# Top-k attention and a hard-swish MLP on one core: another pipeline for the weight conversion, wider PSUM tiles for transposes, another order at the end of a step

## The chip, the cores and the metric

The kernel runs on one core of one Trainium2 chip. The metric is the time of one execution on the device, in microseconds (us). The engines are named as the profile names them: PE (TensorE, with PEld for its weight loads), DVE (VectorE), ACT (ScalarE), POOL (GpSimd) and SP (SyncE, which here only issues DMAs).

## The reference

```python
scores = scale * np.matmul(q, k.transpose(0, 1, 3, 2))          # q, k, v: (8, 8, 576, 64) float32
kth = np.partition(scores, -top_k, axis=-1)[..., -top_k:-top_k + 1]   # top_k = 32
scores = np.where(scores >= kth, scores, -1000000000.0)
attn = np.exp(scores - np.max(scores, axis=-1, keepdims=True))
attn = attn / (np.sum(attn, axis=-1, keepdims=True) + 1e-09)
x = np.matmul(attn, v)            # then (B,H,S,D) -> (4608, 512)
h = x @ w_in                      # w_in (512, 2048) float64
g = h * np.clip(h + 3.0, 0.0, 6.0) / 6.0
out = (g @ w_out).astype(np.float32)     # w_out (2048, 512) float64
```

## The kernel before, in words

The weights arrive as float64, and no engine reads that, so the kernel takes each number as two 32-bit words and puts a float32 together. `convert` does this for one chunk of 128 x 512 numbers, and there are 32 chunks: 16 of `w_in`, then 16 of `w_out`. It loads the words into a tile `st` (two buffers), ACT takes the magnitude of the high word (`Abs`) and scales the low word, POOL clamps, DVE shifts and masks the bits, POOL multiplies and adds, and DVE (`finish`, L125) puts the sign in. `finish` reads `st` too, so `st` is given back only there.

The attention is cut into 160 units: for each of the 8 batches, five tiles of query rows (four of 128, one of 64, the "rest"), and for each tile four pairs of heads. A unit has two rows of 576 scores on each partition (a rest unit has one: the two heads lie on the two halves of the partitions). There is one loop over steps `n`, and all engines take their instructions in the order in which the loop writes them. Step `n` works on several units at once:

- PE computes the scores of unit n+1 into PSUM (`ps`), and ACT copies them to SBUF (`sc`).
- DVE finds the 32 largest of unit n in four rounds, `top(0)` to `top(3)`: each round finds the 8 largest (MAX8), and the first three rounds strike them out (MATCH_REPLACE8).
- POOL masks unit n (`mask`: two passes L246, an add L251, and the shift for the exponential L254).
- ACT does the exponential of unit n-1 (`exp`, L259), and POOL adds a small number to its sums (`den`, L264).
- DVE takes the reciprocal of unit n-2 (L268), ACT scales by it (`weights`, L270), PE transposes the result in nine blocks of 128 x 128 (L282, L291), and ACT copies the blocks to SBUF (`eT`, L284, and `rT`, L410).
- In odd steps PE multiplies two units by v (`values`, L304), and ACT copies the result (`xT`).

Every four units of a query tile make one tile of 128 tokens, and for it `feed_forward` is put on a list. It has eight pieces: four pieces `h` (32 PE passes each, then ACT's relu L329, then a DVE "gate" L333) and four pieces `acc` (the second matmul). `piece()` takes the next one off the list. There are two slots for a piece in a step, one ahead of the transposes and one behind them, and a third in every fourth step. A rest step has one or two.

PSUM has 8 banks. Before, `ps_sc` has 3, `ps_tr` two tiles of 1 bank (the blocks of a unit go through it in two halves, and the transposed k and q of a pair of heads in three parts), `ps_rt` 1 and `ps_w` 2.

Of the kernel before, what the change touches and what calls it, by code (L numbers as in the profile page):

```python
# [11 lines left out]
U32 = mybir.dt.uint32  # L12
PSUM = bass.MemoryType.PSUM
# [12 lines left out]
def kernel(  # L26
# [18 lines left out]
    W2 = 2 * S  # L45
# [14 lines left out]
    rtpool = pool("rt", 2)  # L60
# [7 lines left out]
    ps_tr = pool("ps_tr", 2, space=PSUM)  # L68
    ps_rt = pool("ps_rt", 1, space=PSUM)
# [9 lines left out]
    nc.vector.memset(three[:], 3.0)  # L79
    w_in = const([P, NHP, FF], "w_in")  # L80
# [17 lines left out]

    def convert(dst, src):

        st = stpool.tile([P, 2 * WC], U32, tag="st", name="st")
        nc.sync.dma_start(st[:], src)
        words = st[:].rearrange("p (n two) -> p n two", two=2)
        lo, hi = words[:, :, 0], words[:, :, 1]
        cv = cvpool.tile([P, 3, WC], F32, tag="cv", name="cv")
        a, s, f = cv[:, 0, :], cv[:, 1, :], cv[:, 2, :]
# [22 lines left out]

        return finish  # L130
# [13 lines left out]
    class Pair:  # L144
# [28 lines left out]
        def transpose(self):  # L173
            kT = self.kT = kqpool.tile([P, JP], F32, tag="kT", name="kT")
            qT = self.qT = kqpool.tile([P, S], F32, tag="qT", name="qT")
            for src, dst in ((self.kin, kT[:]), (self.qin, qT[:, 0:JP])):
                ps = ps_tr.tile([P, 512], F32, tag="tr", name="kq")
                for j in range(J):
                    rows = src[:, j, :, :].rearrange("p h d -> p (h d)")
                    nc.tensor.transpose(ps[:, j * P : (j + 1) * P], rows, ident[:])  # L180
                nc.scalar.copy(dst, ps[:, 0:JP])  # L181
            ps = ps_tr.tile([P, 512], F32, tag="tr", name="kq")
            for i, src in enumerate((self.kin, self.qin)):
                rows = src[0:R, J, :, :].rearrange("p h d -> p (h d)")
                nc.tensor.transpose(ps[:, i * R : (i + 1) * R], rows, ident[0:R, 0:R])
            for hh in range(2):
                d = slice(hh * D, (hh + 1) * D)
                nc.scalar.copy(self.kr[d, hh, :], ps[d, 0:R])
            nc.scalar.copy(qT[:, JP:S], ps[:, R : 2 * R])

    class Unit:
# [10 lines left out]
        def scores(self):  # L202
# [5 lines left out]
            sc = self.sc = scpool.tile([P, W2], F32, tag="sc", name="sc")  # L208
# [7 lines left out]
            else:  # L216
                nc.tensor.matmul(ps[:, 0:JP], pr.qT[h0, qs], pr.kT[h0, :])  # L217
                nc.tensor.matmul(ps[:, S + R : 1024], pr.qT[h1, qs], pr.kT[h1, 0 : 1024 - S - R])  # L218
                nc.tensor.matmul(ps[:, 1024:W2], pr.qT[h1, qs], pr.kT[h1, 1024 - S - R : JP])
                nc.tensor.matmul(ps[:, JP : S + R], pr.qT[:, qs], pr.kr[:].rearrange("p h r -> p (h r)"))  # L220
                nc.scalar.copy(sc[:], ps[:, 0:W2])  # L221

# [51 lines left out]
        def transpose(self, rt):  # L274

            sc = self.sc
            eT = self.eT = etpool.tile([P, 2 * J, P], F32, tag="eT", name="eT")

            def blocks(dst, starts):
                ps = ps_tr.tile([P, 512], F32, tag="tr", name="tr")  # L280
                for i, c0 in enumerate(starts):
                    nc.tensor.transpose(ps[:, i * P : (i + 1) * P], sc[:, c0 : c0 + P], ident[:])  # L282
                n = len(starts) * P
                nc.scalar.copy(dst.rearrange("p c q -> p (c q)"), ps[:, 0:n])  # L284

            main = [c * P for c in range(J)]
            blocks(eT[:, 0:J, :], main)
            if self.rest:
                blocks(eT[:, J : J + 2, :], [JP, S - P])
            else:  # L290
                nc.tensor.transpose(rt, sc[:, JP : JP + P], ident[:])  # L291
                blocks(eT[:, J : 2 * J, :], [S + R + c0 for c0 in main])

        def values(self, dst, rT):
# [90 lines left out]
    chunks = [(dst, src) for dst, src in weight_chunks()]  # L385
    finishes = []

    def convert_some(n):
        for dst, src in chunks[:n]:
            finishes.append(convert(dst, src))  # L390
            if len(finishes) > 1:
                finishes.pop(0)()
        del chunks[:n]
        if not chunks:
            while finishes:
# [139 lines left out]
```

## Time and profile before

| what | value |
|---|---|
| median of 3 runs | 2212.35 us (2211.54 to 2212.62) |
| the profiled execution | 2209.28 us |
| its span, first to last instruction | 2207.5 us |
| PE, DVE, ACT, POOL busy | 1697.8, 1612.1, 999.7, 1216.6 us |
| mean granted PE clock | 0.94 of full speed |

Busy times are sums over the whole span; whether an engine sets the end in a stretch is read from the views of that stretch. Everything between the span and the time of the execution (1.8 us) lies outside the program's instructions.

### The profile page before, as it was taken

Reading aid. Unit: us, or ns where it says so; the run is one execution under the profiler, and the core shown is the slowest. Engines: PE = TensorE matmul, PEld = TensorE weight load, DVE = VectorE, ACT = ScalarE, POOL = GpSimd, SP = SyncE. Lnnn points to the kernel's source line nnn. Section 1 sums busy time; section 2 is a strip of 40 time slices with the busy share of each in tenths; the row PEclk is TensorE's granted clock in tenths of the full one; section 3 lists DMA queues with packets and bytes.
Section 4 is the critical chain, followed back from the end, with each engine's and each line's share of the span. In section 5 each row is a group of like instructions: output and inputs, shape, how many; then the busy total and the mean of one; then the engine's idle time right before and its main releaser. Section 6 shows DMA issues by size and latency. Waiting matters only on the chain.

```text
span 2207.5 us, 31292 instructions
## 1 busy us (share of the span) xinstructions
PE 1697.8 (77%) x11904; PEld 1227.9 (56%) x11904; DVE 1612.1 (73%) x3313; ACT 999.7 (45%) x1893; POOL 1216.6 (55%) x918
## 2 busy tenths in 40 slices
PE   3012042588999989898989899988999898988989
PEld 2011032366666666665666666666666666656665
DVE  4555544577888888868888878768888888688880
ACT  2122222244455555544555555544554555445542
POOL 3554544555555656555656565646566665555651
PEclk9975566799999999999999999999999999999999
DMA  4111111101000001001000100001000110000000
GB/s 118 48 38 54 48 39 54 40 6 38 22 22 6 22 26 35 9 17 43 22 6 16 27 22 22 6 22 38 22 6 22 30 34 6 6 6 5 6 6 10
DMA packets 101142, 56.55 MB, mean 26 GB/s; under 512 B 84096, under 2 KB 92288, under 8 KB 100992
## 3 DMA queue, kind: packets, MB, share of 16 engines
q1 hardware_dynamic: 100992, 54.55, 9.1%
q8 instruction: 94, 1.54, 0.3%
q14 instruction: 56, 0.46, 0.1%
HBM read 45.09 MB, written 9.44 MB: 25 GB/s over the span
## 4 chain that ended last, share of the span: by engine, by line
PE 64%; DVE 10%; POOL 9%; issue 8%; ACT 4%; DMA 4%; SPq 0%; ACTq 0%; POOLq 0%
PE h L321 21%; PE acc L340 19%; PE pv L304 7%; PE tr L282 7%; POOL sc L251 4%; POOL wk L246 3%; DVE m L232 3%; PE ps L217 3%; DVE wk L236 3%; PE ps L220 2%; DMA st<-in_moe_w_out_dram 2%; DMA st<-in_moe_w_in_dram 2%; PE ps L218 1%; PE rt L291 1%; DVE w_in L125 1%
## 5 line engine op out<-in xcount | busy, mean ns | idle before, releaser
L246 POOL TENSOR_SCALAR wk<-sc,m 128x576 f32<-128x576 f32 x288 | 636.4, 2218 | 613.2 <-DVE m L232 613.2
L232 DVE MAX8 m<-wk 128x8 f32<-128x576 f32 x864 | 613.0, 746 | 1.6
L282 PE MATMUL tr<-ident,sc 128*128 128x128 f32 x1216 | 195.2, 290 | 467.5 <-issue 390.0
L340 PE MATMUL acc<-w_out,g 128*128 128x512 f32 x1152 | 523.5, 598 | 0.0
L321 PE MATMUL h<-xT,w_in 128*128 128x128 f32 x4096 | 481.5, 276 | 0.0
L321 PEld LDWEIGHTS h<-xT,w_in 128*128 128x128 f32 x4096 | 469.2, 193 | 1.6 <-issue 0.5
L282 PEld LDWEIGHTS tr<-ident,sc 128*128 128x128 f32 x1216 | 147.0, 148 | 533.2 <-issue 472.6
L236 DVE MATCH_REPLACE8 wk<-m,wk 128x576 f32<-128x576 f32 x576 | 423.8, 743 | 0.0
L251 POOL TENSOR_TENSOR sc<-sc,wk 128x1152 f32<-128x1152 f32 (+1 forms) x160 | 382.1, 2388 | 13.3
L340 PEld LDWEIGHTS acc<-w_out,g 128*128 128x128 f32 x1152 | 208.9, 191 | 215.8 <-issue 214.2
L329 ACT ACTIVATE g<-h,three 128x512 f32<-128x512 f32 x144 | 98.9, 687 | 371.6 <-PE h L321 371.6
L270 ACT ACTIVATE sc<-sc,den 128x576 f32<-128x576 f32 x288 | 208.1, 766 | 129.9 <-DVE den L268 129.8
L333 DVE SCALAR_TENSOR_TENSOR g<-g,h 128x512 f32<-128x512 f32 x144 | 98.5, 684 | 194.6 <-ACT g L329 194.6
L284 ACT COPY eT<-tr 128x512 f32<-128x512 f32 x320 | 176.5, 566 | 110.0 <-PE tr L282 101.2
L259 ACT ACTIVATE sc<-sc,shift 128x576 f32<-128x576 f32 x288 | 220.8, 770 | 0.0
L221 ACT COPY sc<-ps 128x1152 f32<-128x1152 f32 x128 | 142.1, 1110 | 159.4 <-PE ps L220 158.4
L232 DVE MAX8 m<-sc 128x8 f32<-128x576 f32 x288 | 203.8, 744 | 13.7 <-ACT sc L221 11.4
L236 DVE MATCH_REPLACE8 wk<-m,sc 128x576 f32<-128x576 f32 x288 | 211.8, 742 | 0.0
L268 DVE RECIPROCAL den<-den 128x2 f32<-128x2 f32 (+1 forms) x160 | 26.0, 162 | 195.6 <-POOL den L264 195.4
L304 PE MATMUL pv<-eT,vm 128*64 128x128 f32 (+1 forms) x2560 | 161.0, 270 | 0.0
L217 PE MATMUL ps<-kT,qT 64*128 64x512 f32 x256 | 151.7, 674 | 0.8 <-ACT qT L181 0.8
L304 PEld LDWEIGHTS pv<-eT,vm 128*64 128x64 f32 x2560 | 133.9, 141 | 13.2 <-issue 9.0
(62 smaller groups left out, 1466.4 us busy)
## 6 DMA issues: line engine op xcount, KB each, us to landing
kin<-in_k_dram SPq DMA_DIRECT2D x64, 128.0 KB, 3.0
qin<-in_q_dram SPq DMA_DIRECT2D x64, 128.0 KB, 2.9
vm<-in_v_dram SPq DMA_DIRECT2D x64, 128.0 KB, 2.3
st<-in_moe_w_in_dram SPq DMA_DIRECT2D x16, 512.0 KB, 3.9
st<-in_moe_w_out_dram SPq DMA_DIRECT2D x16, 512.0 KB, 3.6
out_dram<-o SPq DMA_DIRECT2D x32, 256.0 KB, 2.3
kin<-in_k_dram SPq DMA_DIRECT2D x32, 32.0 KB, 2.6
qin<-in_q_dram SPq DMA_DIRECT2D x32, 32.0 KB, 2.4
```

Source lines behind the costliest of these rows:

```text
L217: nc.tensor.matmul(ps[:, 0:JP], pr.qT[h0, qs], pr.kT[h0, :])
L232: nc.vector.max(self.m[:, t, 8 * r : 8 * r + 8], self.cur[t])
L236: nc.vector.match_replace(wk, self.m[:, t, 8 * r : 8 * r + 8], self.cur[t], LOWEST)
L246: nc.gpsimd.tensor_scalar(self.wk[:, t, :], self.row[t], self.m[:, t, TOP_K - 1 : TOP_K], DROP, ALU.is_lt, ALU.mult,)
L251: nc.gpsimd.tensor_tensor(both, both, self.wk[:, 0:nt, :].rearrange("p t s -> p (t s)"), ALU.add)
L259: nc.scalar.activation(self.row[t], self.row[t], AF.Exp, bias=self.shift[:, t : t + 1], scale=scale, accum_out=self.den[:, t : t + 1],)
L270: nc.scalar.activation(self.row[t], self.row[t], AF.Copy, scale=self.den[:, t : t + 1])
L282: nc.tensor.transpose(ps[:, i * P : (i + 1) * P], sc[:, c0 : c0 + P], ident[:])
L284: nc.scalar.copy(dst.rearrange("p c q -> p (c q)"), ps[:, 0:n])
L304: nc.tensor.matmul(dst[hh * D : (hh + 1) * D, :], pr.vm[:, hh, c, :] if c < J else pr.vr[:, hh, :], rhs, start=(c == 0), stop=(c == J),)
L321: nc.tensor.matmul(h[:, (f - f0) * P : (f - f0 + 1) * P], w_in[:, i, f * P : (f + 1) * P], xT[:, i, :], start=(i == 0), stop=(i == NHP - 1),)
L340: nc.tensor.matmul(acc[:], gs[f // 4][:, (f % 4) * P : (f % 4 + 1) * P], w_out[:, f, :], start=(f == 0), stop=(f == NFC - 1),)
```

## The change

Four things change.

1. **The conversion.** `convert` becomes a generator of two parts with one chunk in flight. The first part loads `st`, has ACT take the magnitude, POOL clamp it, and ACT write the sign (as 2.0 or -2.0) and the scaled low words into PSUM. The second part, one `convert_step()` later, is four DVE operations (shift, xor with the sign, mask, multiply by the low words) and one POOL add, which writes the weights. No instruction of the second part reads `st`. `convert_step()` stands three times in the loop (ahead of `top(1)`, `top(2)` and the end of the step), three times ahead of it, and once more in step 0, instead of three chunks in a row at each step's end.
2. **PSUM for transposes.** `ps_tr` is one tile of 3 banks (`wide()`), one buffer, for the nine blocks of a unit, for the ten transposes of a pair, and for the sign and low words of a chunk. `ps_rt` and the `rT` tile are gone; one ACT copy of 1152 columns takes all nine blocks.
3. **Scores.** Three matmuls per unit instead of four, the narrow one first, and two ACT copies instead of one.
4. **Order.** `weights` (DVE's reciprocal, ACT's two scalings) moves to the head of the step, ahead of `top(0)` and of the first piece. `exp` now stands ahead of `mask` at the end of a step, so POOL's `den` of unit n-1 stands ahead of the mask of unit n. Feed-forward starts at step 6 (8 before), and the third slot is used from step 15 on.

```diff
-ps_tr = pool("ps_tr", 2, space=PSUM)
-ps_rt = pool("ps_rt", 1, space=PSUM)
+ps_tr = pool("ps_tr", 1, space=PSUM)
+    def wide():
+        return ps_tr.tile([P, 3 * 512], F32, tag="tr", name="tr")
     def convert(dst, src):
...
-        nc.scalar.activation(f, lo, AF.Copy, scale=2.0**-52)
         nc.scalar.activation(a, hi.bitcast(F32), AF.Abs)
         nc.gpsimd.tensor_scalar(a, a, HI_MOST, HI_LEAST, ALU.min, ALU.max)
...
-        nc.gpsimd.tensor_tensor(f, f, s, ALU.mult)
-        nc.gpsimd.tensor_tensor(a, a, f, ALU.add)
-        def finish():
-            nc.vector.scalar_tensor_tensor(
-                out=dst.bitcast(U32), in0=hi, scalar=0x80000000, in1=au,
-                op0=ALU.bitwise_and, op1=ALU.bitwise_or,
-            )
+        ps = wide()
+        sign, f = ps[:, 0:WC], ps[:, 512 : 512 + WC]
+        nc.scalar.activation(sign, hi.bitcast(I32), AF.Sign, bias=half[:])
+        nc.scalar.mul(sign, sign, 2.0)
+        nc.scalar.activation(f, lo, AF.Copy, scale=2.0**-52)
+        yield
+        nc.vector.tensor_scalar(au, au, 4, 1, ALU.logical_shift_left, ALU.logical_shift_right)
+        nc.vector.tensor_tensor(au, au, sign.bitcast(U32), ALU.bitwise_xor)
+        nc.vector.tensor_scalar(su, au, 0xFF800000, None, ALU.bitwise_and)
+        nc.vector.tensor_tensor(s, s, f, ALU.mult)
+        nc.gpsimd.tensor_tensor(dst, a, s, ALU.add)
...
+    def convert_step():
+        for c in converting:
+            next(c, None)
+        converting.clear()
+        if chunks:
+            c = convert(*chunks.pop(0))
+            next(c)
+            converting.append(c)
+    FF_FROM = 6
...
+        if d:
+            d.weights()
+        if u:
+            u.begin()
+            u.top(0)
+        run_gate()
...
+        convert_step()
         if n >= FF_FROM:
             piece()
         if u:
             u.top(1)
-        if 2 <= n < NU + 2:
-            units[n - 2].weights()
...
+        if d:
+            d.transpose()
+        convert_step()
...
-        if chunks:
-            convert_some(3)
-        if n >= FF_FROM and two and n % 4 == 3:
+        convert_step()
+        if n > 2 * FF_FROM and two and n % 4 == 3:
             run_gate()
             piece()
+        if 1 <= n < NU + 1:
+            units[n - 1].exp()
...
         if u:
             u.mask()
-        if 1 <= n < NU + 1:
-            units[n - 1].exp()
```

The order of instructions shows this at three places. First DVE in a step of the conversion (steps 1 and 2 of the loop), from the reciprocal on. Before, the three chunks stand behind the last MAX:

```order
L268 RECIPROCAL den<-den 128x2
L232 MAX m<-wk 128x8 x2
L236 MATCH_REPLACE wk<-m,wk 128x576 x2
L232 MAX m<-wk 128x8 x2
L114 TENSOR_SCALAR cv<-cv 128x512
L117 TENSOR_SCALAR cv<-cv 128x512
L120 TENSOR_SCALAR cv<-cv 128x512
L125 SCALAR_TENSOR_TENSOR w_in<-st,cv 128x512
```

And in the changed kernel, from the head of step 2 (L276 is the reciprocal, L240 and L244 are MAX8 and MATCH_REPLACE8, L127 to L130 the second part of a chunk):

```order
L276 RECIPROCAL den<-den 128x2
L240 MAX m<-sc 128x8 x2
L244 MATCH_REPLACE wk<-m,sc 128x576 x2
L127 TENSOR_SCALAR cv<-cv 128x512
L128 TENSOR_TENSOR cv<-cv,tr 128x512
L129 TENSOR_SCALAR cv<-cv 128x512
L130 TENSOR_TENSOR cv<-cv,tr 128x512
L240 MAX m<-wk 128x8 x2
L244 MATCH_REPLACE wk<-m,wk 128x576 x2
L127 TENSOR_SCALAR cv<-cv 128x512
```

The reciprocal went from the middle of the step to its head, and one chunk's four operations stand behind each of three rounds.

Second POOL in a step of the conversion. Before, the mask, then `den`, then the three chunks of the next step:

```order
L246 TENSOR_SCALAR wk<-sc,m 128x576 x2
L251 TENSOR_TENSOR sc<-sc,wk 128x1152
L254 TENSOR_SCALAR shift<-m 128x2
L264 TENSOR_SCALAR den<-den 128x2
L111 TENSOR_SCALAR cv<-cv 128x512
L121 TENSOR_TENSOR cv<-cv 128x512
L122 TENSOR_TENSOR cv<-cv 128x512
L111 TENSOR_SCALAR cv<-cv 128x512
```

In the changed kernel L272 is `den`, L254 to L262 the mask, L131 the add that ends a chunk and L116 the clamp of the next:

```order
L116 TENSOR_SCALAR cv<-cv 128x512
L272 TENSOR_SCALAR den<-den 128x2
L254 TENSOR_SCALAR wk<-sc,m 128x576 x2
L259 TENSOR_TENSOR sc<-sc,wk 128x1152
L262 TENSOR_SCALAR shift<-m 128x2
L131 TENSOR_TENSOR w_in<-cv 128x512
L116 TENSOR_SCALAR cv<-cv 128x512
L131 TENSOR_TENSOR w_in<-cv 128x512
L116 TENSOR_SCALAR cv<-cv 128x512
```

`den` moved ahead of the mask, and a chunk's add and the next chunk's clamp stand behind it.

Third ACT in the steady part, a step with two pieces `h`. Before (L329 is the relu, L270 the scaling):

```order
L259 ACTIVATE sc,den<-sc,shift 128x576 x2
L221 COPY sc<-ps 128x1152
L329 ACTIVATE g<-h,three 128x512
L270 ACTIVATE sc<-sc,den 128x576 x2
L284 COPY eT<-tr 128x512 x2
L329 ACTIVATE g<-h,three 128x512
```

And in the changed kernel (L267 the exponential, L278 the scaling, L326 the relu, L291 the copy of the nine blocks):

```order
L267 ACTIVATE sc,den<-sc,shift 128x576 x2
L225 COPY sc<-ps 128x128
L226 COPY sc<-ps 128x2x512
L278 ACTIVATE sc<-sc,den 128x576 x2
L326 ACTIVATE g<-h,three 128x512
L291 COPY eT<-tr 128x1152
L326 ACTIVATE g<-h,three 128x512
```

The scaling stood behind the relu of the first piece and now stands ahead of it.

## Rows read from the trace of the kernel before

**Rows 1.** Windows: stretch, length, busy us of PE, PEld, DVE, ACT, POOL; PEclk, DMA.
```profile
0.00:414.00 414.00, 99.33 (x557) 74.38 (x557) 203.11 (x362) 106.19 (x196) 195.89 (x168) 0.73 0.19 56
...
555.00:955.00 400.00, 363.55 (x2565) 264.28 (x2563) 333.08 (x705) 206.89 (x391) 240.19 (x162) 1.00 0.08 20
955.00:1023.00 68.00, 61.32 (x458) 40.83 (x459) 46.57 (x94) 33.53 (x70) 33.20 (x39) 1.00 0.07 18
```

**Rows 2.** Timeline of DVE: first round of step 0; end of the conversion, step 11.
```profile
12.21 1.42 DVE L232 MAX8 m<-sc 128x8 f32<-128x576 f32 x2 [11.37 <-ACT sc L221]
...
413.61 0.69 DVE L125 SCALAR_TENSOR_TENSOR w_out<-st,cv 128x512 uint32<-128x512 uint32 x1 [1.15 <-POOL cv L122]
414.22 1.41 DVE L232 MAX8 m<-sc 128x8 f32<-128x576 f32 x2
```

**Rows 3.** Timeline around 105 us (start, duration, engine, line): one chunk, the next's start.
```profile
101.67 0.66 ACT L109 ACTIVATE cv<-st 128x512 f32<-128x512 uint32 x1 [8.16 <-DMA st<-in_moe_w_in_dram]
102.96 0.61 POOL L111 TENSOR_SCALAR cv<-cv 128x512 f32<-128x512 f32 x1 [4.59 <-ACT cv L110]
...
104.58 1.50 POOL L121 TENSOR_TENSOR cv<-cv 128x512 f32<-128x512 f32 x1 [1.01 <-DVE cv L117]
104.88 1.75 DVE L125 SCALAR_TENSOR_TENSOR w_in<-st,cv 128x512 uint32<-128x512 uint32 x1
...
110.60 0.66 ACT L109 ACTIVATE cv<-st 128x512 f32<-128x512 uint32 x1 [7.72 <-DMA st<-in_moe_w_in_dram]
```

**Rows 4.** Timeline, the same step: two DVE rounds, the mask, den, the transposes.
```profile
115.48 1.41 DVE L232 MAX8 m<-sc 128x8 f32<-128x576 f32 x2
116.67 4.41 POOL L246 TENSOR_SCALAR wk<-sc,m 128x576 f32<-128x576 f32 x2
...
118.26 1.41 DVE L232 MAX8 m<-wk 128x8 f32<-128x576 f32 x2
...
124.18 0.22 POOL L264 TENSOR_SCALAR den<-den 128x2 f32<-128x2 f32 x1
...
125.51 1.09 PE L282 MATMUL tr<-ident,sc 128*128 128x128 f32 x4 [31.01 <-issue]
```

**Rows 5.** What PE waited for, 414 us to the end: us in total, times, longest.
```profile
PE tr L282 <- issue: 138.7, 84, 15.6
PE tr L282 <- ACT sc L270: 48.2, 27, 5.4
PE kq L185 <- ACT kT L181: 9.5, 26, 0.4
```

**Rows 6.** Timeline of a steady step: values, scores, piece `h`, what its transposes waited for.
```profile
1714.45 1.09 PE L304 MATMUL pv<-eT,vm 128*64 128x128 f32 x16
...
1716.93 0.69 PE L217 MATMUL ps<-kT,qT 64*128 64x512 f32 x1
...
1718.32 3.74 PE L321 MATMUL h<-xT,w_in 128*128 128x128 f32 x32
...
1721.14 0.17 DVE L268 RECIPROCAL den<-den 128x2 f32<-128x2 f32 x1 [1.69 <-POOL den L264]
...
1722.10 0.69 ACT L329 ACTIVATE g<-h,three 128x512 f32<-128x512 f32 x1 [2.15 <-PE h L321]
...
1722.68 1.43 ACT L270 ACTIVATE sc<-sc,den 128x576 f32<-128x576 f32 x2
...
1723.55 0.63 PE L282 MATMUL tr<-ident,sc 128*128 128x128 f32 x4 [1.49 <-issue]
```

**Rows 7.** Groups by line and shape: busy us, mean ns of one | idle before.
```profile
L259 ACT ACTIVATE sc<-sc,shift 128x576 f32<-128x576 f32 x288 | 220.8, 770 | 0.0
L221 ACT COPY sc<-ps 128x1152 f32<-128x1152 f32 x128 | 142.1, 1110 | 159.4 <-PE ps L220 158.4
L333 DVE SCALAR_TENSOR_TENSOR g<-g,h 128x512 f32<-128x512 f32 x144 | 98.5, 684 | 194.6 <-ACT g L329 194.6
L114 DVE TENSOR_SCALAR cv<-cv 128x512 uint32<-128x512 uint32 x32 | 13.6, 426 | 166.7 <-POOL cv L111 166.7
```

More of the change, by code (lines that the diff above doesn't have):

```diff
@@ L79 @@
     nc.vector.memset(three[:], 3.0)
+    half = const([P, 1], "half")
+    nc.vector.memset(half[:], 0.5)
     w_in = const([P, NHP, FF], "w_in")
@@ L216, in scores @@
             else:
[L217 to L221, printed above, removed]
+                kr = pr.kr[:].rearrange("p h r -> p (h r)")
+                nc.tensor.matmul(ps[:, 1024 : 1024 + 2 * R], pr.qT[:, qs], kr)
+                for hh, d in enumerate((h0, h1)):
+                    nc.tensor.matmul(ps[:, hh * 512 : hh * 512 + JP], pr.qT[d, qs], pr.kT[d, :])
+                nc.scalar.copy(sc[:, JP : JP + 2 * R], ps[:, 1024 : 1024 + 2 * R])
+                nc.scalar.copy(
+                    sc[:].rearrange("p (h s) -> p h s", h=2)[:, :, 0:JP],
+                    ps[:, 0 : 2 * JP].rearrange("p (h s) -> p h s", h=2),
+                )
         def begin(self):
@@ L272, in weights, with transpose, values @@
                 )
[L274 to L294, printed above, removed]
+        def transpose(self):
+            starts = [c * P for c in range(J)]
+            starts += [JP, S - P] if self.rest else [c * P for c in range(J, 2 * J + 1)]
+            eT = self.eT = etpool.tile([P, 2 * J + 1, P], F32, tag="eT", name="eT")
+            ps = wide()
+            for i, c0 in enumerate(starts):
+                nc.tensor.transpose(ps[:, i * P : (i + 1) * P], self.sc[:, c0 : c0 + P], ident[:])
+            n = len(starts)
+            nc.scalar.copy(eT[:, 0:n, :].rearrange("p c q -> p (c q)"), ps[:, 0 : n * P])
+        def values(self, dst):
             pr, eT = self.pair, self.eT
@@ L383, in run_gate @@
         gate = None
[L385 to L395, printed above, removed]
-                finishes.pop(0)()
-    FF_FROM = 8
+    chunks = list(weight_chunks())
+    converting = []
+    def convert_step():
[7 more added lines that the diff above has]
+    FF_FROM = 6
     state = {}
@@ L406, in values @@
         pv = ps_w.tile([P, 512], F32, tag="w", name="pv")
-        rT = None
-        if not rest:
-            rT = rtpool.tile([P, 2, P], F32, tag="rT", name="rT")
-            nc.scalar.copy(rT[:].rearrange("p u q -> p (u q)"), state["rt"][:, 0 : 2 * P])
         for i, u in enumerate((u0, u1)):
-            u.values(pv[:, i * w : (i + 1) * w], None if rest else rT[:, i, :])
+            u.values(pv[:, i * w : (i + 1) * w])
         hp0 = u0.pair.hp
@@ L445 @@
     pairs[0, 0].load()
-    pairs[0, 1].load()
+    convert_step()
     pairs[0, 0].transpose()
     units[0].scores()
+    pairs[0, 1].load()
+    convert_step()
+    convert_step()
     pairs[0, 1].transpose()
@@ L462 @@
             p.load()
-        if u:
-            u.begin()
-            u.top(0)
-        run_gate()
+        convert_step()
         if n >= FF_FROM:
@@ L470 @@
             u.top(1)
-        if 2 <= n < NU + 2:
-            units[n - 2].weights()
-            d = units[n - 2]
-            if not d.rest and (n - 2) % 2 == 0:
-                state["rt"] = ps_rt.tile([P, 512], F32, tag="rt", name="rt")
-            d.transpose(None if d.rest else state["rt"][:, ((n - 2) % 2) * P : ((n - 2) % 2 + 1) * P])
+        if d:
+            d.transpose()
+        convert_step()
         if u:
@@ L484 @@
             p.transpose()
-        if n >= 2 and n < NU + 2 and (n - 2) % 2 == 1:
+        if d and (n - 2) % 2 == 1:
             values(n - 2)
```

43 lines of the change are left out of this document (19 added, 24 removed).

## The prediction

> **What bounds the kernel now.** I read the windows first, to find stretches with different limits. Until 414 us PE is busy for 99 of 414 us, DVE for 203 and POOL for 196 [rows 1]: no engine is full, so this stretch is made of waiting. From 555 to 955 us PE is busy for 364 of 400 us and DVE for 333: PE sets the end there, and what can be won is PE's idle time. The rest steps from 955 to 1023 leave PE idle for 6.7 us; there are four such stretches.
>
> The first stretch is the conversion. Step 0's first round begins at 12.2 us and step 11's at 414.2 us, just behind the last chunk [rows 2]: eleven steps in 402 us, 36.5 each. The timeline shows a chunk going through ACT, POOL, DVE and POOL one after the other [rows 3]: ACT starts at 101.67, DVE's last part ends at 106.63, and only then can the next transfer into that `st` begin; ACT takes that chunk up at 110.60, 4.0 us later. Three chunks in a row at 9 us, and then DVE's rounds, the mask and the transposes, in which no chunk moves, make the 36 us. PE stood idle for 31 us ahead of its transposes [rows 4].
>
> For the steady part I read what PE waits for. From 414 us on PE is idle ahead of L282 and L185 for 138.7 + 48.2 + 9.5 us; the longest wait, 15.6, still belongs to the last step of the conversion, and without it 181 us stay [rows 5]. A step's timeline shows why [rows 6]: PE ends piece `h` at 1722.06, ACT then does the relu (1722.10) and only behind it the scaling (1722.68), and PE starts its transposes at 1723.55, after 1.49 us. The reciprocal had been there at 1721.3; the scaling stood in ACT's queue behind a relu that waits for PE itself.
>
> **The conversion, step by step.** DVE's own work per step would be 10 us of rounds (three at 118.26 - 115.48 = 2.78 and one of 1.4 [rows 4]) and three second parts. One of these is two operations like L114 (0.43) and two with an operand in PSUM like L333 (0.68) [rows 7], so 2.2 us; together 16.7. But one 3-bank tile now carries chunks and transposes, and I expect this loop from `den` to `den`:
> - POOL's mask as now, from 116.67 to 124.18: 7.5; behind it the add of the chunk in flight, like L121, 1.5, and the next clamp, 0.6 [rows 3, 4]: 9.6.
> - DVE's second part of this chunk 2.2; only then is the tile free for nine transposes (four take 1.09 [rows 4], so some 2.1); ACT's copy of 1152 columns 1.1 [rows 7]; Sign, doubling and low words of the next chunk, three passes like L109, 2.0 [rows 3]; its second part 2.2, which is longer than the rounds beside it; three passes of the third chunk 2.0.
> - Two exponentials 1.6 [rows 7], which stand behind these passes on ACT, and `den` 0.2.
>
> That is 23.0, and 23.7 with some 0.08 for each of nine handoffs (124.18 + 0.22 to the next engine's start is of that size). The next reciprocal waits for this `den`, and DVE's first round stands behind it.
>
> One cost more is unsure. L125 takes 1.75 us in rows 3 and 0.69 in rows 2, where POOL has nothing to do; in rows 3 it ends 0.55 after POOL's L121. So it was held until POOL's operation ended. The change's operations beside the mask have only one SBUF source each. If they aren't held the price is nothing; if each of two is held by a pass of 2.2, DVE loses up to 4.4, of which 1.5 is covered (the rounds reach the next chunk 8.1 after `den`, POOL's clamp ends at 9.6). I take 1.3, nearer to the row that shows a hold of 1.06. A step is 25 us.
>
> The Trainium skill (SBUF — State Buffer, "Who interferes with whom") says that DVE and GpSimd share a port pair as an exclusive lock for the length of an instruction, and that tensor_scalar in a two-port mode takes it too, not only operations with two SBUF inputs. By it L127 and L129 are held, the upper end of that bound (2.9 a step, some 13 us more over eight steps); by the rows alone, which show only the two-input kind held, nothing, some 10 us less. No row here shows a tensor_scalar held.
>
> Steps 2, 4, 5 and 8 take 25 each. In 3 and 7 a pair's ten transposes (2.3, by the rate of rows 4), `values` (2.5, from 1714.45 to 1716.93 [rows 6]) and two ACT operations (1.0) stand ahead of the third chunk's Sign: 31. Step 6 has a relu in that place, 26; in step 9 the chunks end, 24. Sum 212. Ahead of them, step 0's rounds must wait for chunks 0 and 1, since pair 0's transposes need the tile: 12.2 + 4.0 transfer + 2.6 + 2.2 for the one, 4.6 for the other and some 3 of queueing, 29 (now 12.2, so this is a loss). Steps 0 and 1 pass seven chunks (4.4 each) and three pairs' transposes with their copies (4.4 each) through the tile, and chunk 3's load stands behind twenty loads on SP (some 14): 58. So step 10 begins near 299, step 11 near 308 instead of 414: **-106**. Bounds: -190 if DVE's 16.7 set every step from 2 on and step 0 loses only 10; -50 with holds at their upper end and 4 us more of handoffs a step.
>
> **Pieces done earlier.** By step 11 feed-forward has done ten pieces instead of six (two in each of the steps 6 to 10, against 8 to 10). A piece takes PE 3.45 us back to back (3.74 with its tail [rows 6]), and PE bounds what follows: 4 x 3.45 = **-14**.
>
> **The steady part.** With the scaling ahead of the relu, and `den` ahead of the mask, the 181 us are open. But the reciprocal at the head of the step now waits for an exponential that ACT reaches only behind the end of PE's last step (`values`, xT copy). From that end: exp 0.3 to 1.9, `den`, reciprocal 2.3; scores' copies on ACT until 3.2; half the scaling done at 4.0. PE has scores (1.4 [rows 6]) and a piece (3.45) to do until 4.8, so these cover it with 0.8 to spare, and nearly nothing in the step where DVE, with a gate, is 1 us later. DVE follows PE by 2.3 instead of leading it. PE's 364 us of work against DVE's 333 in the same 400 [rows 1] leave PE the bound.
>
> What stays of the 181: the rest steps' 27 (four times 6.7 [rows 1]), which I leave as they are; a new wait of 1.1 once in four steps, where the second slot is empty and `values` follows the transposes with only the copy of 1152 columns between (29 groups: 32); and 10 for tight places. 181 - 27 - 32 - 10: **-112**. Bounds: -150 if the copy is covered by a late piece and the places aren't tight; 0 if the exponential comes late in every step.
>
> Scores cost PE the same (two 512-column matmuls on two halves of the rows beside each other, one narrow), and the second ACT copy is hidden since ACT is busy for 207 of 400 us [rows 1]. The pair's transposes lose their 9.5 us wait, which is in the 181.
>
> **Sum.** 2209.3 (the profiled execution: span 2207.5 and 1.8 around it) - 106 - 14 - 112 = 1977. The median of the runs is 3 above the profiled one, so I say **1980**, with 1925 to 2045 for this case alone.
>
> **Rivals.**
> - The conversion is bound by DVE, 17 us a step: 80 less in the first stretch, about 1895. For it: two `st` buffers free early hide the transfers. Against: the chain above goes through one tile. Chance 0.13.
> - The steady part wins nothing, since DVE, held at the head of each step, makes the scaling late by the 1 us that was won: about 2090. For it: margins of 0.8 and near 0. Chance 0.18.
> - The conversion saves nothing, because chunks and transposes take turns in one tile at 36 us a step; the steady part gains: about 2085. Against: the loop would need 12 us that I can't find. Chance 0.05.
> - Slower: the reciprocal at the head locks DVE behind PE and PE behind the scaling. It decides only if each of 149 steps takes 1.6 us longer than I say, 13.1 instead of 11.5. The loop from PE's end over exp, reciprocal, scaling (4.1), transposes 1.3, piece 3.45, `values` 2.5 is 11.3, and POOL's loop (mask 7.5, exp 1.6, `den`) 9.4, so neither reaches it. Chance 0.03; at its point 2213 and more.
>
> **Chances.** Forecast 0.60, the four rivals 0.39, no change 0.01. Within 0.2% is what a measurement of this kernel can't tell from no change; faster 0.96, same 0.01, slower 0.03. The range takes in the DVE-bound case below and the two of 2085 to 2090 above: 1890 to 2090.
>
> **What would show it.** Step 11's first MAX8 near 308 (250 to 350); in the conversion DVE idle ahead of the reciprocal for some 3 to 4 us a step, and ahead of L127 waiting for POOL's clamp; PE's transposes L289 waiting for DVE's L130. In the steady part L278 ahead of L326 on ACT, PE's idle time behind step 11 down from 181 to about 70, mostly ahead of L301 and none of the 1.49 kind ahead of L289; DVE idle ahead of L276 about 2 us in some steps. The forecast is wrong if PE still waits for L278 in most steps, or if the tile's turns cost more than the transfers did.

## The result, and the profile after

| what | before | after |
|---|---|---|
| median of 4 runs, side by side | 2211.94 us | 1949.32 us (1948.64 to 1949.51) |
| ratio, 95% interval | | 0.881 (0.880 to 0.883) |
| the profiled span | 2207.5 us | 1946.8 us |
| step 11's first MAX8 | 414.2 us | 299.5 us |
| from there to the end | 1793.3 us | 1647.3 us |

The change is faster by 11.9%. 1980 was predicted, within 1890 to 2090. The first stretch gave 114.7 us (106 predicted), the part behind step 11 gave 146.0 (112 + 14 predicted).

The loop of the conversion can be read link by link where [rows 3] and [rows 4] stood before. Timeline of the changed kernel, steps 2 to 3 of the loop (start, duration, engine, line):

```profile
86.05 0.22 POOL L272 TENSOR_SCALAR den<-den 128x2 f32<-128x2 f32 x1 [1.73 <-ACT sc L267]
...
93.83 1.26 POOL L131 TENSOR_TENSOR w_in<-cv 128x512 f32<-128x512 f32 x1
...
95.18 0.61 POOL L116 TENSOR_SCALAR cv<-cv 128x512 f32<-128x512 f32 x1
95.83 0.43 DVE L127 TENSOR_SCALAR cv<-cv 128x512 uint32<-128x512 uint32 x1 [1.27 <-POOL cv L116]
...
97.54 0.69 DVE L130 TENSOR_TENSOR cv<-cv,tr 128x512 f32<-128x512 f32 x1
...
98.38 2.15 PE L289 MATMUL tr<-ident,sc 128*128 128x128 f32 x9 [24.18 <-DVE cv L130]
...
100.57 1.12 ACT L291 COPY eT<-tr 128x1152 f32<-128x1152 f32 x1 [6.74 <-PE tr L289]
...
106.07 0.72 ACT L120 ACTIVATE tr<-st,half 128x512 f32<-128x512 int32 x1 [1.36 <-DVE cv L130]
...
108.00 0.76 ACT L267 ACTIVATE sc<-sc,shift 128x576 f32<-128x576 f32 x1
...
109.69 0.22 POOL L272 TENSOR_SCALAR den<-den 128x2 f32<-128x2 f32 x1 [1.73 <-ACT sc L267]
109.95 0.17 DVE L276 RECIPROCAL den<-den 128x2 f32<-128x2 f32 x1 [3.91 <-POOL den L272]
```

From `den` to `den` it is 23.64 us. The mask, the add and the clamp take 9.74 of them, the second part 2.44, the transposes 2.2, the copy 1.1; then come Sign (from 102.15), the second part of the next chunk, the third chunk's passes (106.07), the exponentials (108.00) and `den`. DVE stands still for 3.91 ahead of the reciprocal, as the forecast said. What the engines waited for before 299 us (line waited at, releaser: us in total, times, longest):

```profile
PE tr L289 <- DVE cv L130: 129.2, 8, 24.2
...
DVE cv L127 <- POOL cv L116: 49.8, 16, 12.1
```

The part behind step 11 in windows (length, then busy us of PE, PEld, DVE, ACT, POOL), first the kernel before, which answers to [rows 1]:

```profile
414.22:2207.50 1793.28, 1598.50 (x11347) 1153.51 (x11347) 1408.75 (x2952) 893.50 (x1697) 1020.46 (x751) 0.99 0.07 19
```

and the changed kernel:

```profile
299.50:1946.80 1647.30, 1560.69 (x11036) 1118.66 (x11035) 1402.46 (x2951) 877.87 (x1599) 1018.58 (x750) 0.99 0.07 20
```

PE's idle time falls from 194.8 to 86.6 us, and its busy time by 37.8. The 194.8 holds 8.7 of the conversion's last wait (15.6 in [rows 5]): it ends at 422.93, and this stretch begins at 414.22. What PE waits for behind 299 us in the changed kernel, to be set against [rows 5]:

```profile
PE pv L301 <- DVE g L330: 43.1, 30, 2.3
PE tr L289 <- ACT sc L278: 21.2, 4, 5.3
PE h L318 <- DVE g L330: 17.2, 29, 1.8
PE tr L289 <- issue: 1.0, 2, 0.8
PE pv L301 <- ACT eT L291: 0.6, 4, 0.2
```

The waits of the kind in [rows 6] (1.49 ahead of the transposes) are gone: 1.0 us in all is left. The 21.2 are the four stretches of rest steps. But 60.3 us are waits for DVE's gate L330, which the forecast did not name, and the wait for the copy into `eT`, which it put at 32, is 0.6. The timeline of the changed kernel shows both, and the new order on ACT:

```profile
935.99 0.69 DVE L330 SCALAR_TENSOR_TENSOR g<-g,h 128x512 f32<-128x512 f32 x1
...
936.73 1.09 PE L301 MATMUL pv<-eT,vm 128*64 128x128 f32 x16 [1.17 <-DVE g L330]
...
947.51 1.15 PE L289 MATMUL tr<-ident,sc 128*128 128x128 f32 x9
...
948.50 3.60 PE L337 MATMUL acc<-w_out,g 128*128 128x512 f32 x8
...
957.92 1.09 PE L301 MATMUL pv<-eT,vm 128*64 128x128 f32 x16
958.03 1.12 ACT L291 COPY eT<-tr 128x1152 f32<-128x1152 f32 x1 [0.39 <-PE tr L289]
...
959.20 1.09 PE L301 MATMUL pv<-eT,vm 128*64 128x128 f32 x16
...
960.12 0.39 PE L301 MATMUL pv<-eT,vr 128*64 128x128 f32 x4
...
962.79 0.17 DVE L276 RECIPROCAL den<-den 128x2 f32<-128x2 f32 x1 [1.30 <-POOL den L272]
...
963.40 1.45 ACT L278 ACTIVATE sc<-sc,den 128x576 f32<-128x576 f32 x2
...
965.59 1.15 PE L289 MATMUL tr<-ident,sc 128*128 128x128 f32 x9
965.79 0.69 ACT L326 ACTIVATE g<-h,three 128x512 f32<-128x512 f32 x1 [0.94 <-PE h L318]
```

`values` (L301) starts at 957.92, ahead of the copy, with the earlier of its two units; the copy is done at 959.15, just as it needs the later one (959.20). At 936.73 it waits for PSUM instead: `ps_w` has two buffers, and the one with a piece `h` comes free only with the gate, which stands on DVE behind `top(2)`'s strike. From the end of `values` at 960.51 the reciprocal starts 2.28 us later (962.79), ACT scales at 963.40, ahead of the relu (965.79), and PE starts the transposes at 965.59 without a gap.

### The profile page after: what moved, and what is told of

It is laid out like the page before. It is cut to its first block, busy times and chain, and to the rows that moved or that the text cites. A ratio compares the mean times of both kernels' runs of the same rounds, so it can differ in the third digit from the quotient of the medians.

```text
span 1946.8 us, 30583 instructions
## 1 busy us (share of the span) xinstructions
PE 1669.4 (86%) x11648; PEld 1197.8 (62%) x11648; DVE 1589.9 (82%) x3314; ACT 1025.2 (53%) x1861; POOL 1156.9 (59%) x886
## 3 DMA queue, kind: packets, MB, share of 16 engines
q1 hardware_dynamic: 100992, 54.55, 10.3%
## 4 chain that ended last, share of the span: by engine, by line
PE 36%; DVE 26%; POOL 20%; issue 14%; ACT 4%; SPq 1%; DMA 0%; POOLq 0%; DVEq 0%; ACTq 0%
PE acc L337 14%; DVE m L240 11%; POOL wk L254 10%; DVE wk L244 10%; PE h L318 8%; POOL sc L259 7%; PE pv L301 5%; PE tr L289 4%; PE ps L223 2%; DVE g L330 2%; PE ps L214 1%; ACT sc L267 1%; DVE cv L128 1%; DVE cv L130 1%; POOL den L272 1%
## 5 line engine op out<-in xcount | busy, mean ns | idle before, releaser
L254 POOL TENSOR_SCALAR wk<-sc,m 128x576 f32<-128x576 f32 x288 | 636.1, 2216 | 34.6 <-DVE m L240 17.4
L240 DVE MAX8 m<-wk 128x8 f32<-128x576 f32 x864 | 616.0, 751 | 2.7
L337 PE MATMUL acc<-w_out,g 128*128 128x512 f32 x1152 | 529.2, 603 | 0.0
L318 PEld LDWEIGHTS h<-xT,w_in 128*128 128x128 f32 x4096 | 469.2, 193 | 55.0 <-DVE g L330 32.8
L318 PE MATMUL h<-xT,w_in 128*128 128x128 f32 x4096 | 489.5, 278 | 10.3 <-DVE g L330 10.3
L244 DVE MATCH_REPLACE8 wk<-m,wk 128x576 f32<-128x576 f32 x576 | 424.6, 745 | 0.0
L259 POOL TENSOR_TENSOR sc<-sc,wk 128x1152 f32<-128x1152 f32 (+1 forms) x160 | 383.0, 2394 | 13.4
L337 PEld LDWEIGHTS acc<-w_out,g 128*128 128x128 f32 x1152 | 208.3, 190 | 261.2 <-issue 259.3
L272 POOL TENSOR_SCALAR den<-den 128x2 f32<-128x2 f32 (+1 forms) x160 | 35.3, 221 | 559.0 <-ACT sc L267 559.0
L289 PE MATMUL tr<-ident,sc 128*128 128x128 f32 x1344 | 184.4, 284 | 151.4 <-DVE cv L130 129.2
L289 PEld LDWEIGHTS tr<-ident,sc 128*128 128x128 f32 x1344 | 162.2, 147 | 203.1 <-issue 172.3
L291 ACT COPY eT<-tr 128x1152 f32<-128x1152 f32 (+1 forms) x160 | 168.8, 1055 | 175.4 <-PE tr L289 174.9
L276 DVE RECIPROCAL den<-den 128x2 f32<-128x2 f32 (+1 forms) x160 | 25.7, 161 | 253.0 <-POOL den L272 252.7
L326 ACT ACTIVATE g<-h,three 128x512 f32<-128x512 f32 x144 | 99.0, 688 | 253.1 <-PE h L318 253.1
L267 ACT ACTIVATE sc<-sc,shift 128x576 f32<-128x576 f32 x288 | 220.7, 769 | 11.6 <-POOL shift L262 11.6
L278 ACT ACTIVATE sc<-sc,den 128x576 f32<-128x576 f32 x288 | 210.4, 778 | 22.0 <-DVE den L276 21.6
L244 DVE MATCH_REPLACE8 wk<-m,sc 128x576 f32<-128x576 f32 x288 | 212.1, 744 | 0.0
L301 PE MATMUL pv<-eT,vm 128*64 128x128 f32 (+1 forms) x2560 | 172.9, 282 | 43.7 <-DVE g L330 43.1
L240 DVE MAX8 m<-sc 128x8 f32<-128x576 f32 x288 | 203.2, 743 | 0.0
L301 PEld LDWEIGHTS pv<-eT,vm 128*64 128x64 f32 x2560 | 141.7, 148 | 65.1 <-DVE g L330 47.6
L226 ACT COPY sc<-ps 128x1024 f32<-128x1024 f32 x128 | 130.1, 1016 | 0.0
```

Of the source, the lines that this page charges most:

```text
L240: nc.vector.max(self.m[:, t, 8 * r : 8 * r + 8], self.cur[t])
L244: nc.vector.match_replace(wk, self.m[:, t, 8 * r : 8 * r + 8], self.cur[t], LOWEST)
L254: nc.gpsimd.tensor_scalar(self.wk[:, t, :], self.row[t], self.m[:, t, TOP_K - 1 : TOP_K], DROP, ALU.is_lt, ALU.mult,)
L259: nc.gpsimd.tensor_tensor(both, both, self.wk[:, 0:nt, :].rearrange("p t s -> p (t s)"), ALU.add)
L267: nc.scalar.activation(self.row[t], self.row[t], AF.Exp, bias=self.shift[:, t : t + 1], scale=scale, accum_out=self.den[:, t : t + 1],)
L278: nc.scalar.activation(self.row[t], self.row[t], AF.Copy, scale=self.den[:, t : t + 1])
```

## The experiments

The theory: the order of exp, mask and scaling gives the steady part, and needs both of its halves (scaling at the head, `den` ahead of the mask); the new conversion gives the first stretch, whose loop runs through the 3-bank tile. The rivals: that the steady part's gain comes from the wider tile or from the conversion's end, and that the loop of the conversion is set by something else than the tile. The changed kernel and twelve variants, with ratios to runs of the kernel before on the same chip:

| kernel | median us | ratio (95%) | step 11 at | from there | PE busy there |
|---|---|---|---|---|---|
| after | 1949.3 | 0.881 (0.880 to 0.883) | 299.5 | 1647.3 | 1560.7 |
| e1_old_order | 2055.4 | 0.930 (0.928 to 0.931) | 278.8 | 1775.4 | 1592.1 |
| e2_weights_late | 2051.9 | 0.928 (0.927 to 0.930) | 293.9 | 1756.1 | 1585.8 |
| e3_mask_first | 2765.1 | 1.251 (1.249 to 1.253) | 336.3 | 2426.9 | 1781.0 |
| e4_order_only | 2029.6 | 0.918 (0.917 to 0.919) | 367.4 | 1661.4 | 1578.1 |
| e5_gate_early | 1916.6 | 0.867 (0.866 to 0.868) | 300.7 | 1613.8 | 1552.3 |
| e6_words_in_sbuf | 1911.3 | 0.865 (0.863 to 0.866) | 260.9 | 1647.0 | 1559.2 |
| e7_both | 1872.8 | 0.847 (0.846 to 0.849) | 257.1 | 1613.8 | 1552.6 |
| e8_ff_from_8 | 1957.5 | 0.886 (0.884 to 0.887) | 301.0 | 1654.3 | 1571.6 |
| e9_exp_early | 1861.7 | 0.842 (0.841 to 0.843) | 245.8 | 1613.9 | 1553.7 |
| e10_old_first | 1903.7 | 0.861 (0.860 to 0.862) | 288.0 | 1613.9 | 1552.9 |
| e11_old_first_sbuf | 1870.4 | 0.846 (0.845 to 0.847) | 255.0 | 1613.9 | 1554.3 |
| e12_exp_early_alone | 1935.3 | 0.875 (0.874 to 0.877) | 288.0 | 1645.4 | 1560.3 |

### The order taken apart: e1 to e4

e1_old_order: the changed kernel with the order of before.

```diff
-        if d:
-            d.weights()
         if u:
             u.begin()
...
         if d:
+            d.weights()
             d.transpose()
...
-        if 1 <= n < NU + 1:
-            units[n - 1].exp()
         if u:
             u.mask()
+        if 1 <= n < NU + 1:
+            units[n - 1].exp()
```

> The changed kernel with the old order of a step: the scaling (reciprocal, ACT) behind top(1) and the first piece, the mask ahead of the exponential; conversion, PSUM tiles and scores as in the change. Theory (the steady part's gain comes from the order alone): the first stretch keeps its gain (step 11 near 300 to 315 us), PE's idle time behind it is back at about 180 us, so 2085 us (2060 to 2110). Rival (the gain comes from the wide tile, the single copy and the three-matmul scores): 1950 to 1985.

The steady part falls back to 1775.4 us, against 1793.3 before and 1647.3 after, and PE's idle time in it to 183.3, as expected. The total, 2055.4, lies 5 us below the range, since the first stretch is shorter than expected. Timeline of e1, with the wait of [rows 6]:

```profile
956.50 0.69 ACT L326 ACTIVATE g<-h,three 128x512 f32<-128x512 f32 x1 [2.28 <-PE h L318]
957.09 1.43 ACT L278 ACTIVATE sc<-sc,den 128x576 f32<-128x576 f32 x2
957.95 1.38 PE L289 MATMUL tr<-ident,sc 128*128 128x128 f32 x9 [1.49 <-issue]
...
959.17 3.74 PE L318 MATMUL h<-xT,w_in 128*128 128x128 f32 x32
```

So all that is not the order brings 18 of the 146, and 8.7 of the 18 are the conversion's last wait. PE's waits in e1 have no row for a gate (L330): the waits for gates come with the new order. PE's busy time counts too. Behind the wait the nine transposes take 1.22 us (957.95 to 959.17), since the second half of the scaling ends only at 958.52; in the changed kernel they took 0.99 (947.51 to 948.50). So part of what PE waited for is counted as busy. Windows of L289 alone (length, busy us of PE and PEld), in e1:

```profile
278.80:2054.20 1775.40, 188.00 (x1265) 139.20 (x1263) 0.99 0.07 18
```

and in the changed kernel, 21.9 us less for as many transposes:

```profile
299.50:1946.80 1647.30, 166.08 (x1263) 146.93 (x1263) 0.99 0.07 20
```

These groups overlap others, so they don't add up to the 31.4 by which PE's whole busy time differs; `values` (L301) goes the other way, 176.83 in e1 and 184.89 in the changed kernel.

The first stretch is a surprise: step 11 is reached at 278.8, 20.7 us earlier than with the new order.

e2_weights_late: `exp` ahead of `mask` stays, only the scaling goes back behind `top(1)` (the upper half of the diff above).

> The changed kernel with only the scaling moved back behind top(1) and the first piece; the exponential stays ahead of the mask. Theory (ACT's scaling behind the relu is what PE waits for): the 1.49 us waits ahead of the transposes come back in three of four steps, some 90 to 110 us, so 2040 to 2060. Rival (the order of exponential and mask alone wins it): 1945 to 1970.

1756.1 us behind step 11, and 2051.9 in all, as expected: `den` ahead of the mask alone wins little. Step 11 is reached at 293.9: of the 20.7 us that the new order costs the first stretch, the exponential's place alone takes 15.1, and the scaling's place the other 5.6. e3_mask_first is the other half: the scaling stays at the head, `exp` goes back behind `mask` (the lower half of the diff).

> The changed kernel with only the mask put back ahead of the exponential; the scaling stays at the head of a step. Theory (the reciprocal at the head waits for den, so den must not stand behind the mask): DVE waits 7.5 us more at the head of each two-row step, 9.75 of work plus 7.7 instead of about 11.5: 6 to 7 us for each of 117 steps, so 2600 to 2800. Rival (the two moves are independent, the mask is hidden): 1945 to 1975.

2765.1 us, as expected. The reciprocal at the head now waits for a `den` behind the mask, and every two-row step is locked: 17.0 to 18.2 us a step against 10.3 to 14.4. Timeline of e3:

```profile
1240.02 0.17 DVE L276 RECIPROCAL den<-den 128x2 f32<-128x2 f32 x1 [7.20 <-POOL den L272]
...
1249.26 4.41 POOL L254 TENSOR_SCALAR wk<-sc,m 128x576 f32<-128x576 f32 x2 [9.27 <-DVE m L240]
...
1257.02 0.17 DVE L276 RECIPROCAL den<-den 128x2 f32<-128x2 f32 x1 [7.20 <-POOL den L272]
```

DVE's rounds and POOL's mask take turns: 17.0 us from reciprocal to reciprocal, and PE is not in this loop. So this is a lock, but not the one of the forecast's slower rival, whose loop goes over PE and ACT. (PE's mean granted clock behind step 11 is 0.85 here and 0.99 in the changed kernel, and nine transposes take 2.15 us at 1241.09 against 1.15 at 947.51. This lengthens PE's busy time in the table.) e4_order_only puts the new order alone into the kernel before.

```diff
         if p:
             p.load()
+        if 2 <= n < NU + 2:
+            units[n - 2].weights()
...
-        if 2 <= n < NU + 2:
-            units[n - 2].weights()
...
-        if u:
-            u.mask()
         if 1 <= n < NU + 1:
             units[n - 1].exp()
+        if u:
+            u.mask()
```

> The kernel before with only the new order: scaling at the head of a step, exponential ahead of the mask; old conversion, old PSUM tiles, old scores, feed-forward from step 8. Theory: the steady part gains 120 to 145 us as in the change, the first stretch stays at about 400 us, so 2070 to 2095. Rival (the order needs the wide tile): 2180 to 2215.

With narrow tiles the steady part is 1661.4: the order gives 132 of the 146, and brings 49.5 us of waits for gates with it. It shortens the old conversion as well, to step 11 at 367.4, some 32 us a step against 36.5, which I had not expected and which makes the whole, 2029.6, 40 us less than the range. Order and conversion work against each other there: alone the order saves 47 us of the first stretch, all the rest (e1) saves 135, and both together 115.

### The gates: e5

```diff
         if d:
             d.transpose()
+        run_gate()
         convert_step()
         if u:
             u.top(2)
-        run_gate()
```

> The changed kernel with the second gate of a step put behind top(1) instead of top(2) on DVE, so that the PSUM buffer of a piece h comes free 2.8 us earlier. Theory (PE's 60 us of waiting for DVE's gates is waiting for one of the two buffers of ps_w): most of it goes, 30 to 45 us, so 1905 to 1920. Rival (DVE is by now the bound, and PE will wait elsewhere): 1943 to 1952.

33.5 us behind step 11 are won, within the range; step 11 is reached 1.2 later. PE's waits in e5 behind 300 us:

```profile
PE tr L289 <- ACT sc L278: 21.2, 4, 5.3
PE h L318 <- DVE g L330: 14.3, 30, 1.1
PE acc L337 <- DVE g L330: 11.3, 15, 0.8
...
PE pv L301 <- ACT eT L291: 0.6, 4, 0.2
```

The 43.1 us ahead of L301 are gone, and part of them stands in smaller waits behind. Of the 33.5, 25.1 are idle time of PE and 8.4 its busy time. So the gate's place on DVE held `ps_w`, and through it PE.

### The tile: e6 and e7

e6_words_in_sbuf leaves the transposes in the 3-bank tile and puts a chunk's sign and low words into SBUF.

```diff
-        cv = cvpool.tile([P, 2, WC], F32, tag="cv", name="cv")
+        cv = cvpool.tile([P, 3, WC], F32, tag="cv", name="cv")
...
-        ps = wide()
-        sign, f = ps[:, 0:WC], ps[:, 512 : 512 + WC]
+        sign, f = s, cv[:, 2, :]
```

> The changed kernel with the sign and the low words in SBUF instead of the 3-bank PSUM tile (three slices of cv instead of two). Theory (in the conversion, chunks and transposes take turns in one tile, and that makes a step 23.6 us): steps of 17 to 19 us, step 0 begins near 12 instead of 28, together 45 to 75 us less, 1875 to 1905. Rival (handoffs and the mask set the step, or DVE operations with two SBUF sources are held by POOL): 1935 to 1955.

Step 11 is reached at 260.9, 38.6 us earlier, and the time is 1911.3 us, between the two ranges. That is what the tile's turns cost, less what the words in SBUF cost DVE (last section): 4.8 ahead of step 0, 8.8 in step 0, 8.9 in step 3, where a pair's transposes pass through it, and 1 to 4 in each of the other steps up to step 9. A step is still 21.7 us, not DVE's 17, and step 0 begins at 23.6, not 12, so the rival "bound by DVE" was not near. e7_both joins e5 and e6:

> Both edits together, the earlier gate and the words in SBUF. Theory: the gains are in different stretches and add up, 1835 to 1870. Rival (either edit alone wins nothing): 1940 to 1955.

The gains of 32.7 and 38.0 add up, and a little more: 76.5. Of the 5.8 more, 3.8 come in the first stretch (step 11 at 257.1 against e6's 260.9). The time, 1872.8, is 2.8 above the range.

### The pieces: e8

```diff
-    FF_FROM = 6
+    FF_FROM = 8
```

> The changed kernel with feed-forward from step 8 again (the third slot from step 19 on). Theory (the pieces done early in the conversion, where PE is idle, are worth their PE time): 10 to 16 us more, 1959 to 1966. Rival (empty slots later take them up for nothing): 1946 to 1953.

1957.5 us, between the two ranges: the four pieces are worth 8.1 us. Behind step 11 the passes of the pieces themselves grow by 15.1 us (L318 from 524.36 to 533.21, L337 from 513.47 to 519.76), but PE's whole busy time by only 10.9, and its idle time falls by 3.9, from 86.6 to 82.7. Step 11 itself begins 1.5 later.

### What the order costs the conversion: e9 to e12

e9_exp_early is e7 with `exp` ahead of the last conversion step.

```diff
+        if 1 <= n < NU + 1:
+            units[n - 1].exp()
         convert_step()
         if n > 2 * FF_FROM and two and n % 4 == 3:
             run_gate()
             piece()
-        if 1 <= n < NU + 1:
-            units[n - 1].exp()
```

> The kernel of e7 (gate early, words in SBUF) with exp(n-1) put on ScalarE ahead of the last conversion step of a piece, so that it and the sum behind it no longer stand behind the third chunk's passes. If these queues set the step of the first stretch: 2 to 4 us less a step, twelve steps, 1840 to 1860 us. Rival, that the mask's wait or another one sets the step, so that exp's place does nothing: 1868 to 1877 us. The part behind step 11 stays at 1614 us in both.

1.3 us a step, fewer than I said (20.5 against 21.8), and 1861.7 us, 1.7 above the range and the fastest kernel here. Waits of e9 from 30 to 255 us:

```profile
DVE cv L126 <- POOL cv L116: 31.2, 11, 3.3
ACT cv L115 <- POOL w_in L130: 27.1, 7, 6.1
```

By these waits the chain now goes over POOL: the add behind the mask frees the buffer `cv`, then the clamp, then DVE. No run cuts this chain, so that it sets the step is not shown. In e7 the waits of DVE for that clamp came to 8.5 us in the same stretch. Next, the old order for the conversion's units only:

```diff
-        if d:
+        late = n < 9
+        if d and not late:
             d.weights()
...
         if d:
+            if late:
+                d.weights()
             d.transpose()
...
-        if 1 <= n < NU + 1:
+        if 1 <= n < NU + 1 and not late:
             units[n - 1].exp()
...
         if u:
             u.mask()
+        if 1 <= n < NU + 1 and late:
+            units[n - 1].exp()
```

on e5 (e10) and on e7 (e11).

> The kernel of e5 (gate early) with the old order, scaling and mask, for the units of the conversion (n < 9), the new order behind them. If the order of exp and mask costs the conversion what e1 showed (step 11 at 278.8 us with the old order, 299.5 with the new), the time is 1892 to 1902 us, with step 11 near 280. Rival, that the gate's new place has taken up that time already: 1912 to 1920 us.

> The kernel of e7 (gate early, words in SBUF) with the old order for the units of the conversion (n < 9), the new order behind them. If the order's price in the conversion is still there: 1850 to 1865 us, step 11 near 240. Rival, that with the words in SBUF another queue sets the step: 1868 to 1877 us, step 11 near 257.

e10 wins 12.9 us and no more (1903.7, 1.7 above the range): the steps are 22.1 long against 23.7, as in e1, but the step that changes from the old order to the new takes 35.7 against 25.0 in e5. In e11 that step takes 30.8 against 22.1, the others win some 1 each, and the whole wins 2.4 us: the rival's range. e12 then makes e9's edit in the changed kernel, with the words in PSUM:

> The changed kernel with one edit: exp(n-1) stands ahead of the last conversion step of a piece. If den's place behind the third chunk's three ACT passes is what the new order costs the conversion (e1: 20.7 us by step 11), the chain from mask to mask loses some 2 us (of the 3.8 that den comes earlier, the add and the clamp on POOL take back 1.9): step 11 at 277 to 290 us instead of 299.5, the time 1927 to 1940 us. Rival, that the turns of the 3-bank tile set the step whatever exp does: step 11 at 297 to 302 us, the time 1946 to 1952 us. The part behind step 11 stays at 1647 us in both.

Step 11 at 288.0 and 1935.3 us, as said. In e12's timeline `den` no longer waits for the third chunk's passes (L120 at 104.42 is that chunk's Sign; compare 106.07 and 109.69 above):

```profile
104.04 0.22 POOL L272 TENSOR_SCALAR den<-den 128x2 f32<-128x2 f32 x1 [2.81 <-ACT sc L267]
...
104.42 0.69 ACT L120 ACTIVATE tr<-st,half 128x512 f32<-128x512 int32 x1
```

That is 11.5 of the 20.7 us by which e1's first stretch is shorter. The other 9.2 stay open. By e2, 5.6 of the 20.7 came with the scaling's place; whether they are part of the 9.2 no run shows.

## Why the prediction was right, step by step

**The first stretch** came out by the chain that was written down. Step 0 began at 28.4 (29 predicted); steps 0 and 1 took 58.0 (58); steps 2, 4, 5 and 8 took 23.6, 23.6, 23.7 and 25.0 (25 each); 3 and 7 took 30.6 and 29.7 (31), 6 took 23.7 (26), 9 took 22.8 (24). The 23.7 of links and handoffs was the step itself. What was too much is mainly the 1.3 for holds and the relu in step 6: step 10 at 289.2 instead of 299. e6 shows by cutting it that the tile is a link of this loop, and e12 that `den`'s place behind the third chunk is another.

**The holds** were small. L129 took 20.2 us in all against L127's 13.7, with the same shape: 6.5 us in 32 chunks, 4.8 of them in two instructions (the other 1.7 in six that took 0.71). One of the two, and a piece of the pass that held nothing, in the changed kernel's timeline:

```profile
86.37 4.41 POOL L254 TENSOR_SCALAR wk<-sc,m 128x576 f32<-128x576 f32 x2
...
89.15 0.44 DVE L127 TENSOR_SCALAR cv<-cv 128x512 uint32<-128x512 uint32 x1
...
90.35 0.71 DVE L129 TENSOR_SCALAR cv<-cv 128x512 uint32<-128x512 uint32 x1
...
216.16 2.61 POOL L259 TENSOR_TENSOR sc<-sc,wk 128x1152 f32<-128x1152 f32 x1
216.22 2.83 DVE L129 TENSOR_SCALAR cv<-cv 128x512 uint32<-128x512 uint32 x1
```

At 216.22 a tensor_scalar of DVE is held by POOL's whole add of two SBUF inputs; at 89.15 one runs its usual 0.44 in the middle of POOL's passes. The prediction's rule from the Trainium skill (SBUF — State Buffer, "Who interferes with whom"), that a tensor_scalar in a two-port mode and POOL exclude each other, agrees with the first and not with the second, if L127 and L129 run in such a mode, which no run here shows. So the upper end of 2.9 a step was not reached.

The prediction also misread a row. It says that POOL had nothing to do while L125 took 0.69 us at 413.61 [rows 2]; the trace of the kernel before has POOL's mask there:

```profile
413.56 4.93 POOL L246 TENSOR_SCALAR wk<-sc,m 128x576 f32<-128x576 f32 x2
```

POOL had just begun it, and its two passes took 4.93 instead of their usual 4.41: here POOL lost 0.5 and L125 nothing. So [rows 3] and [rows 2] compare POOL's two-input operation L121 with its mask pass, and not a busy POOL with an idle one.

The steps of 23.6 and 23.7 pay nothing for holds, as the prediction's lower bound has it, but for another reason: what L127 and L129 meet there is mostly the mask pass, which holds them little or not at all (last section). Step 8, which has one of the two long holds, took 25.0.

**The pieces** (-14 predicted): -8.1 by e8. The size of the work was right (15.1 us against 13.8). What failed is "PE bounds what follows": with the pieces back behind step 11, 4.2 us go from PE's other busy time and 3.9 from its waits, so PE is not the bound in every step.

**The steady part** was right in its mechanism and wrong in three terms. That the scaling stood behind the relu, and that moving it needs `den` ahead of the mask, is shown by e1 to e4: `exp` ahead of the mask alone (e2) wins 19 us behind step 11 over the old order (e1), the scaling at the head alone (e3) loses some 650, and both win 128. The chain from the end of `values` to the scaling came out as written, too: 2.28 us to the reciprocal (2.3 predicted). Of the 181 us of PE's waits 83 stayed (the sum of the five rows in the section on the result), where 69 were predicted. The terms:
- the wait of `values` for the 1152-column copy, 32 predicted: 0.6. The step that failed is "only the copy of 1152 columns between": `values` does the earlier unit first (1.28 us from 957.92 to 959.20), and the copy, 1.12, lies beside it. The two groups of L304 could have been seen in the kernel before.
- rest steps, 27 predicted: 21.2.
- tight places, 10 predicted: 60.3 of waits for gates. The forecast had DVE follow PE by 2.3 and a gate late by 1 us, but did not ask which buffer the gate gives back. e5 settles it: with the gate moved, 33.5 us come back.
- not predicted: PE's busy time fell by 37.8 us, where only the pieces' 14 were forecast. The transposes alone were busy 21.9 less than with the old order, since no late scaling stretches them (e1).
- counted in neither term: 8.7 us of the conversion's last wait, which lay behind 414.2.

So the gates cost 50 us more than the forecast had for tight places, and the absent copy wait (31), the busy time (24), the last wait (9) and the rest steps (6) went the other way. That the part behind step 11 came out only 20 us off is in part luck.

**The rivals.** The conversion bound by DVE: no, DVE idles 3.91 a step ahead of the reciprocal, and with the tile's turns gone (e6) a step is 21.7. The steady part wins nothing: no, 146.0 us. The locked step: no, its loop over PE and ACT did not set the step; 1647.3 us for 149 steps is 11.1 a step, and it needed 13.1. A lock over DVE and POOL exists (e3, 1.25 times the time of before), and the change avoids it by the place of `exp`.

## What to carry to other kernels

When an instruction moves to the head of a queue, its inputs may have to move ahead of the long work as well: here one half of the change gains next to nothing, and the other half alone makes the kernel a quarter slower than before. When a step is made tighter, list for each engine which buffers its late instructions give back (here a gate on DVE that frees a PSUM bank for PE), and put those instructions first. A tile that two pipelines share makes them take turns: here room in SBUF gave back 38.6 us.

## What the runs showed of the hardware that was not expected

Whether DVE was held went by what POOL ran, not by DVE's own operation alone. POOL's add of two SBUF inputs (L259, L258 in e6) held DVE: a tensor_scalar with one SBUF input (512 uint32 columns) took 2.83 us instead of 0.43, twice, when the add had started 0.06 us before (2.84 and 2.85 in e6), and in e6 a chunk's last multiply, which has two SBUF inputs there, took 2.97 to 2.99 us instead of 0.69, six times. That raises the multiply's mean in e6 to 1.13 us. With its second input in PSUM the same multiply took 0.69 beside the same add, six times in the changed kernel.

POOL's mask pass (L254, L253 in e6), a tensor_scalar, held almost nothing: L127 took 0.42 to 0.44 us in it all nine times, and in e6 an exclusive-or with two SBUF inputs took 0.69 in it all nine times, as without POOL. The pass, too, kept its 4.41 or 4.42 us for two in all these steps but step 1, where it took 4.57. The most that any of these lost beside the pass is 0.35 us, once. Timeline of e6:

```profile
92.87 4.42 POOL L253 TENSOR_SCALAR wk<-sc,m 128x576 f32<-128x576 f32 x2
...
96.13 0.69 DVE L127 TENSOR_TENSOR cv<-cv 128x512 uint32<-128x512 uint32 x1
...
97.37 2.67 POOL L258 TENSOR_TENSOR sc<-sc,wk 128x1152 f32<-128x1152 f32 x1
97.60 2.99 DVE L129 TENSOR_TENSOR cv<-cv 128x512 f32<-128x512 f32 x1
```

Why POOL's two operations differ stays open. Even so e6 is the faster kernel: the holds cost less than the tile's turns.

In all traces here the words of the weights are read as f32, uint32 and int32; whether an engine could read float64 itself, no run tried.
